# Attention and two MLP layers on one core: the order of the MLP part handed to the framework's scheduler

## The chip, the cores and the metric

The kernel runs on one core of a Trainium2 chip. The metric is the device time of one execution in microseconds. A core has five engines that matter here: TensorE (PE, matmuls; PEld is its weight load), VectorE (DVE), ScalarE (ACT), GpSimd (POOL), and SyncE (SP), which here only issues DMA transfers. Each works through its own queue of instructions in order, and waits for the others through semaphores.

## What is computed

Sigmoid attention over 4 batches and 12 heads (S = 448, D = 64), then two MLP layers over 1792 tokens, all in fp32. The weights come as fp64 and are read as 64-bit integers.

```python
def _attn_ref(q, k, v):
    scores = q @ k.T / sqrt(64) - log(S)
    return sigmoid(scores) @ v
def _moe_ref(x, w_in, w_out):            # x: 1792 x 768, w_in: 768 x 2048, w_out: 2048 x 768
    h = x @ w_in
    r = np.maximum(h, 0.0)
    return (r * r) @ w_out
def _moe2_ref(x, w_in, w_out, alpha):
    h = x @ w_in
    g = np.maximum(h, 0.0) + alpha * np.minimum(h, 0.0)
    return g @ w_out
x = attention, transposed to 1792 x 768
out = _moe2_ref(_moe_ref(x, ...), ...)
```

## The kernel before

Attention takes the first 158.6 us; the MLP part is what the change touches. It runs in 32 units, n = 0 to 31: two layers, in each two halves of the tokens (p), in each 8 blocks of 256 columns of d_ff (fp). fp32 values are split into a high and a low word, and a product takes three matmuls (high by high, high by low, low by high).

A unit has two phases on TensorE. First come seven products of a Strassen-like scheme (`product(k)`, L396): 9 matmuls of 448 columns each, into three PSUM banks h0, h1, h2 in the order 0, 1, 2, 1, 2, 0, 1. ACT copies h0 to c21 (L588). The adds (L582, DVE) combine h1 and h2 with c21 into c12, c22 and c21, and a product may overwrite a bank only after its add has read it: product 3 needs the first add on h1, which needs c21. `hidden` then makes the activation g as two words: in layer 0 on ACT (relu L403, square L404, L405), in layer 1 on ACT (L411, L412), DVE (L415) and ACT (L416); the low word is DVE's L417. Then come the output products (`out_products`, L434), in pairs on two PSUM tiles o0 and o1: 72 matmuls of 448 columns in layer 0, 84 of 384 in layer 1. Each pair is collected by DVE into acc (L469; on ACT, L467, in the first block), and only then its tile can be written again.

Beside that each unit prepares later ones. The weights of the next unit: four sums (`weight_sum`, L123 to L129, DVE), then high words on ACT (L136) and low words on DVE (L137) of four pieces, called s12, a1, a2 and s34 (s12 and s34 are made of sums, a1 and a2 of words_i). The output weights: high word L495 (ACT), low word L499 (POOL, four pieces). Raw weights are loaded from DRAM (L86, L88, issued by SP) into two buffers called raw, scaled in two steps (L94, L96, ACT), joined into words_i or words_o (L103, DVE), and kept in DRAM (L105); later units recall them (L111). All raw weights, of both layers, are loaded and joined in attention and in units 0 to 14. The next half of the tokens is staged: ACT L158 and POOL L159 write a piece into the one `stage` tile, SP stores it (L505, kept_x), and units 7, 15 and 23 load it back as X. POOL also makes x sums (L151).

All code, attention and MLP, stands in one `with tc.manual_schedule():` block: the instructions of each engine run in the order in which the code issues them. The MLP code sets that order by hand: `at(step, ...)` puts a side job into one of 13 steps (i0 to i6 behind the seven products, o0 to o5 behind the output pairs), and `do(step)` issues it there.

Of the kernel before, what the change touches and what calls it, by code (L numbers as in the profile page):

```python
# [20 lines left out]
def fused_kernel(ctx: ExitStack, tc: tile.TileContext, q, k, v, w1i, w1o, w2i, w2o, alpha, out):  # L21
# [142 lines left out]
    with tc.manual_schedule():  # L164
# [206 lines left out]


        mpool = ctx.enter_context(tc.tile_pool(name="mpool", bufs=1, reuse_waits="tile"))
        psum = ctx.enter_context(tc.tile_pool(name="mpsum", bufs=1, space=bass.MemoryType.PSUM, reuse_waits="tile"))
        X.append(mpool.tile([P, 2, KH, S], F32R, name="x6"))
        e21, e22, e12, e11 = (mpool.tile([P, S], F32, name=f"c{s}") for s in ("21", "22", "12", "11"))
        pos = [mpool.tile([P, S], F32, name=f"pos{i}") for i in range(2)]
        WO = [mpool.tile([P, 2, DM], F32R, name=f"wo{j}") for j in range(2)]
        G = [mpool.tile([P, 2, PAIR], F32R, name=f"g{j}") for j in range(2)]
        acc.append(mpool.tile([P, NC * PAIR], F32, name="acc1"))  # L380
        stage = mpool.tile([P, 2, S], F32R, name="stage")
        two = [psum.tile([P, 2, 512], F32, name="o0")]
        hb = [psum.tile([P, 512], F32, name=f"h{i}") for i in range(3)]
        two.append(psum.tile([P, 2, 512], F32, name="o1"))
        BANK = (0, 1, 2, 1, 2, 0, 1)
        OPERAND = (0, 4, 3, 5, 6, 1, 2)
        HIGH, LOW = ((0, 0), (0, 1)), ((1, 0),)
        turns = {"pair": 0, "pos": 0, "x": 0}

        def product(k):  # L390

            ps = hb[BANK[k]][:, :S]
            for c in range(KH):
                at = OPERAND[k] * HALF + c * P
                for i, (wp, xp) in enumerate(((0, 0), (0, 1), (1, 0))):
                    nc.tensor.matmul(ps, W[:, wp, at:at + P], X[k][:, xp, c], start=(k < 3 and c == 0 and i == 0), stop=(c == KH - 1 and i == 2), skip_group_check=True)  # L396

        def hidden(n, src, e, j, t):

            layer, p, fp = UNITS[n]  # L400
            gh, gl = (G[j][:, i, t * S:(t + 1) * S] for i in range(2))
            if layer == 0:
                nc.scalar.activation(e, src, AF.Relu)  # L403
                nc.scalar.activation(gh, e, AF.Square)  # L404
                nc.scalar.activation(e, e, AF.Square)  # L405
                second = lambda: None
            else:
                f = 2 * fp + j
                up = pos[turns["pos"] % 2]
                turns["pos"] += 1  # L410
                nc.scalar.activation(up, src, AF.Relu)  # L411
                nc.scalar.activation(e, src, AF.Relu, scale=-1.0)  # L412

                def second():
                    nc.vector.scalar_tensor_tensor(out=e, in0=e, scalar=nal[:, f:f + 1], in1=up, op0=ALU.mult, op1=ALU.add)  # L415
                    nc.scalar.activation(gh, e, AF.Copy)  # L416
            return second, lambda: nc.vector.tensor_sub(gl, e, gh)  # L417

        def outputs(n):

            if UNITS[n][0] == 0:
                return [[(c, t), (c + 1, t)] for t in (1, 0) for c in range(0, NC, 2)]
            return [[(m, 0), (m, 1)] for m in reversed(range(NM))]

        def out_product(n, o, ps, j, ways, begin, end):

            for i, (gi, wi) in enumerate(ways):
                if UNITS[n][0] == 0:
                    c, t = o
                    ops = WO[j][:, wi, c * P:(c + 1) * P], G[j][:, gi, t * S:(t + 1) * S]  # L430
                else:
                    m, e = o
                    ops = G[j][:, gi, m * P:(m + 1) * P], WO[j][:, wi, e * HALF:(e + 1) * HALF]
                nc.tensor.matmul(ps, *ops, start=(begin and i == 0), stop=(end and i == len(ways) - 1), skip_group_check=True)  # L434

        def out_products(n):

            size = S if UNITS[n][0] == 0 else HALF
            pairs = []
            for os in outputs(n):  # L440
                both = two[turns["pair"] % 2][:, :, :size]
                turns["pair"] += 1
                pairs.append((os, both))
            for ways in (HIGH, LOW):
                for os, both in pairs[:2]:
                    for i in range(2):
                        out_product(n, os[i], both[:, i], 1, ways, ways is HIGH, False)
            for at, (os, both) in enumerate(pairs):
                for i in range(2):
                    if at < 2:  # L450
                        out_product(n, os[i], both[:, i], 0, HIGH + LOW, False, True)
                    else:
                        out_product(n, os[i], both[:, i], 0, HIGH + LOW, True, False)
                        out_product(n, os[i], both[:, i], 1, HIGH + LOW, False, True)
                collect(n, os, both)
                yield at

        def collect(n, os, both):
            layer, p, fp = UNITS[n]
            if layer == 0:  # L460
                c, t = os[0]
                part = values_of(p)[:, c:c + 2, t]
            else:
                m = os[0][0]
                part = acc[p][:, m * DM:(m + 1) * DM].rearrange("p (e c) -> p e c", e=2)
            if fp == 0:
                nc.scalar.activation(part, both, AF.Copy)  # L467
            else:
                nc.vector.tensor_add(part, both, part)  # L469
            if fp == NB - 1 and layer == 1:  # L470
                if n == NU - 1:
                    for e in range(2):
                        store(p * PAIR + m * P, acc[p][:, m * DM + e * HALF:m * DM + (e + 1) * HALF], slice(e * HALF, (e + 1) * HALF), (nc.sync, nc.scalar))
                else:
                    store(p * PAIR + m * P, acc[p][:, m * DM:(m + 1) * DM])

        def store(col, rows, channels=slice(0, DM), queues=(nc.sync,)):

            i = at_queue = 0
            while i < P:  # L480
                b, at = divmod(col + i, S)
                to = out[b * S:(b + 1) * S, channels]
                if at < MAIN:
                    r, p = divmod(at, P)
                    n = min(P - i, P - p)
                    to = to[:MAIN].rearrange("(p r) c -> p r c", r=R)[p:p + n, r, :]
                else:
                    n = min(P - i, S - at)
                    to = to[at:at + n, :]
# [17 lines left out]
        for n in range(NU):  # L507
# [8 lines left out]
            def do(step):  # L516
                for job in todo.get(step, ()):
                    job()
# [134 lines left out]
```

## Time and profile before

| | |
|---|---|
| median of 3 runs | 1223.83 us (1223.69 to 1228.6) |
| the profiled execution | 1226.25 us, span 1224.5 us, mean granted clock 0.968 |
| TensorE matmuls busy | 1105.6 us (90%) |
| DVE / ACT / POOL busy | 772.1 / 604.8 / 274.8 us |
| L396, product matmuls | 2016, busy 435.9 us |
| L434, output matmuls | 1344 of 384 columns, busy 271.5 us; 1152 of 448 columns, busy 252.5 us; 48 of the latter take 9.99 us in a row |
| L495 (ACT) and L499 (POOL), mean of one | 836 ns, 1226 ns |

The difference between the profiled execution's time and its span, 1.75 us, lies around the span. A wait of an engine is the idle time right before an instruction, with what ended it. Idle time of an engine that is not the bottleneck costs nothing by itself.

### The profile page before, as it was taken

Reading aid. Unit: us, or ns where it says so; the run is one execution under the profiler, and the core shown is the slowest. Engines: PE = TensorE matmul, PEld = TensorE weight load, DVE = VectorE, ACT = ScalarE, POOL = GpSimd, SP = SyncE. Lnnn points to the kernel's source line nnn. Section 1 sums busy time; section 2 is a strip of 40 time slices with the busy share of each in tenths; the row PEclk is TensorE's granted clock in tenths of the full one; section 3 lists DMA queues with packets and bytes.
Section 4 is the critical chain, followed back from the end, with each engine's and each line's share of the span. In section 5 each row is a group of like instructions: output and inputs, shape, how many; then the busy total and the mean of one; then the engine's idle time right before and its main releaser. Section 6 shows DMA issues by size and latency. Waiting matters only on the chain.

```text
span 1224.5 us, 14729 instructions
## 1 busy us (share of the span) xinstructions
PE 1105.6 (90%) x5607; PEld 932.5 (76%) x5607; DVE 772.1 (63%) x990; ACT 604.8 (49%) x933; POOL 274.8 (22%) x229
## 2 busy tenths in 40 slices
PE   9999999889898789888889899899899899999998
PEld 5555578778787678777678788788788888888888
DVE  5458866577677556657666646666665646656664
ACT  5577767555455576555454554333332352333332
POOL 0012212323423022323423212231322211101011
PEclk9999999899899989989899999999999999999999
DMA  7677455455656755656556412221226411111102
GB/s 155 152 199 198 148 196 167 165 173 166 199 164 220 282 208 196 220 193 225 199 199 217 172 52 97 67 82 63 73 69 247 142 52 40 41 50 52 52 26 90
DMA packets 126006, 174.77 MB, mean 143 GB/s; under 512 B 55536, under 2 KB 98800, under 8 KB 124272
## 3 DMA queue, kind: packets, MB, share of 16 engines
q1 hardware_dynamic: 123440, 172.59, 43.5%
q10 hardware_dynamic: 2496, 1.25, 0.4%
q8 instruction: 44, 0.72, 0.2%
q14 instruction: 26, 0.21, 0.1%
HBM read 123.87 MB, written 49.94 MB: 142 GB/s over the span
## 4 chain that ended last, share of the span: by engine, by line
PE 37%; DVE 25%; ACT 19%; DMA 12%; issue 5%; POOL 1%; SPq 1%; ACTq 0%; DVEq 0%
PE o L434 17%; PE h L396 11%; DMA kept_x<-stage 4%; ACT wi L136 4%; PE av L265 3%; DVE c L582 3%; DVE c L415 3%; PE sc L245 3%; DVE sums L125 3%; DVE acc L469 3%; DVE wi L137 2%; ACT g L416 2%; DVE g L417 2%; ACT g L404 2%; ACT c L412 2%
## 5 line engine op out<-in xcount | busy, mean ns | idle before, releaser
L396 PE MATMUL h<-x,wi 128*128 128x448 f32 x2016 | 435.9, 377 | 34.1 <-DVE c L582 34.1
L396 PEld LDWEIGHTS h<-x,wi 128*128 128x128 f32 x2016 | 390.5, 194 | 74.1 <-DVE c L582 37.5
L434 PE MATMUL o<-wo,g 128*128 128x384 f32 x1344 | 271.5, 355 | 45.6 <-DVE acc L469 27.6
L434 PEld LDWEIGHTS o<-wo,g 128*128 128x128 f32 x1344 | 245.5, 199 | 70.1 <-ACT wi L136 25.3
L434 PE MATMUL o<-g,wo 128*128 128x448 f32 x1152 | 252.5, 371 | 32.2 <-DVE acc L469 19.2
L434 PEld LDWEIGHTS o<-g,wo 128*128 128x128 f32 x1152 | 211.6, 188 | 70.4 <-DVE acc L469 20.1
L499 POOL TENSOR_TENSOR wo<-words_o,wo 128x384 fp32r<-128x384 f32 x128 | 152.7, 1226 | 354.9 <-ACT wo L495 354.7
L469 DVE TENSOR_TENSOR acc<-o,acc 128x768 f32<-128x768 f32 (+1 forms) x182 | 184.5, 1015 | 73.3 <-PE o L434 72.0
L582 DVE TENSOR_TENSOR c<-h,c 128x448 f32<-128x448 f32 x160 | 98.9, 618 | 144.4 <-PE h L396 83.2
L137 DVE TENSOR_TENSOR wi<-sums,wi 128x768 fp32r<-128x768 f32 x64 | 61.2, 957 | 109.5 <-ACT wi L136 109.5
L159 POOL TENSOR_TENSOR stage<-acc,stage 128x448 fp32r<-128x448 f32 x36 | 41.2, 1145 | 363.0 <-ACT stage L158 363.0
L417 DVE TENSOR_TENSOR g<-c,g 128x448 fp32r<-128x448 f32 x128 | 88.7, 693 | 3.6 <-ACT g L416 1.9
L588 ACT ACTIVATE c<-h 128x448 f32<-128x448 f32 x32 | 17.2, 538 | 148.5 <-PE h L396 137.8
L247 ACT ACTIVATE a<-sc,bias 128x896 f32<-128x896 f32 x72 | 69.1, 1005 | 35.6 <-PE av L265 22.6
L416 ACT ACTIVATE g<-c 128x448 fp32r<-128x448 f32 x64 | 37.0, 578 | 78.0 <-DVE c L415 77.9
L137 DVE TENSOR_TENSOR wi<-words_i,wi 128x768 fp32r<-128x768 f32 x64 | 48.4, 757 | 40.2 <-ACT wi L136 40.2
L403 ACT ACTIVATE c<-c 128x448 f32<-128x448 f32 x48 | 27.5, 573 | 73.8 <-DVE c L582 73.8
L411 ACT ACTIVATE pos<-c 128x448 f32<-128x448 f32 x48 | 27.2, 568 | 73.5 <-DVE c L582 73.5
L158 ACT ACTIVATE stage<-acc 128x448 fp32r<-128x448 f32 x36 | 20.5, 571 | 84.8 <-DMA kept_x<-stage 84.8
L265 PE MATMUL av<-a,v 128*64 128x448 f32 x288 | 59.4, 548 | 0.0
L151 POOL TENSOR_TENSOR acc<-acc 128x448 f32<-128x448 f32 x40 | 57.3, 1450 | 0.1
L136 ACT ACTIVATE wi<-sums 128x768 fp32r<-128x768 f32 x64 | 53.0, 829 | 0.0
(166 smaller groups left out, 989.5 us busy)
## 6 DMA issues: line engine op xcount, KB each, us to landing
kept_x<-stage SPq DMA_DIRECT2D x36, 448.0 KB, 2.9
x<-kept_x SPq DMA_DIRECT2D x12, 1344.0 KB, 8.4
v<-in_v_dram SPq DMA_DIRECT2D x24, 192.0 KB, 2.9
nat<-in_q_dram SPq DMA_DIRECT2D x22, 192.0 KB, 3.5
nat<-in_k_dram SPq DMA_DIRECT2D x20, 192.0 KB, 3.3
late<-held SPq DMA_DIRECT2D x12, 224.0 KB, 2.2
acc<-late SPq DMA_DIRECT2D x1, 2688.0 KB, 9.4
out_dram<-acc SPq DMA_DIRECT2D x14, 192.0 KB, 2.7
```

The costliest lines, as they stand in the source:

```text
L136: nc.scalar.activation(hi, w, AF.Copy)
L137: nc.vector.tensor_sub(lo, w, hi)
L151: eng.tensor_sub(to[c], x[c], y[c])
L247: nc.scalar.activation(sig[u, j], ps[:, :, :S], AF.Sigmoid, bias=bias[:, :1], scale=SCALE)
L265: nc.tensor.matmul(avs[u][h * D:(h + 1) * D, :S], vals[u][:, h, j, :], a[:, h, :], start=(u % 2 == 0 and j == 0), stop=(u % 2 == 1 and j = ...
L396: nc.tensor.matmul(ps, W[:, wp, at:at + P], X[k][:, xp, c], start=(k < 3 and c == 0 and i == 0), stop=(c == KH - 1 and i == 2), skip_group ...
L416: nc.scalar.activation(gh, e, AF.Copy)
L417: return second, lambda: nc.vector.tensor_sub(gl, e, gh)
L434: nc.tensor.matmul(ps, *ops, start=(begin and i == 0), stop=(end and i == len(ways) - 1), skip_group_check=True)
L469: nc.vector.tensor_add(part, both, part)
L499: nc.gpsimd.tensor_sub(WO[j][:, 1, at], words["o"][:, j, at], WO[j][:, 0, at])
L582: nc.vector.tensor_add(to, hb[bank][:, :S], other)
```

## The change

The `manual_schedule` block now ends with attention. The MLP code stands outside it, with one indentation less and otherwise unchanged, so the framework's scheduler sets the order of every engine's queue there. The instructions and their number stay the same; the line numbers behind line 371 go down by one (L396 becomes L395, L469 L468, and so on).

```diff
@@ -369,257 +369,256 @@
             values(2 * ND - 1)
             finish(2 * ND - 1)
 
-
-        mpool = ctx.enter_context(tc.tile_pool(name="mpool", bufs=1, reuse_waits="tile"))
-        psum = ctx.enter_context(tc.tile_pool(name="mpsum", bufs=1, space=bass.MemoryType.PSUM, reuse_waits="tile"))
...
+    mpool = ctx.enter_context(tc.tile_pool(name="mpool", bufs=1, reuse_waits="tile"))
+    psum = ctx.enter_context(tc.tile_pool(name="mpsum", bufs=1, space=bass.MemoryType.PSUM, reuse_waits="tile"))
...
```

DVE, a unit of layer 1 before, from the second add on h1 to the second accumulation (c_1787 is c22, c_1788 c12, c_1789 c11, c_1786 c21; the first L137 is s12, the second a1):

```order
L582 TENSOR_TENSOR c_1787<-h_1800,c_1787 128x448
L127 TENSOR_TENSOR sums<-words_i 128x384
L129 TENSOR_TENSOR sums<-words_i,sums 128x384
L582 TENSOR_TENSOR c_1788<-h_1801,c_1788 128x448
L415 SCALAR_TENSOR_TENSOR c_1787<-c_1787,nal,pos_1790 128x448
L137 TENSOR_TENSOR wi<-sums,wi 128x768
L417 TENSOR_TENSOR g_1795<-c_1787,g_1795 128x448
L415 SCALAR_TENSOR_TENSOR c_1788<-c_1788,nal,pos_1791 128x448
L582 TENSOR_TENSOR c_1786<-h_1800,c_1786 128x448
...
L469 TENSOR_TENSOR acc_76<-o_1802,acc_76 128x768
...
L137 TENSOR_TENSOR wi<-words_i,wi 128x768
L469 TENSOR_TENSOR acc_76<-o_1798,acc_76 128x768
```

The same place now (all numbers one higher: c_1788 is c22, c_1789 c12, c_1790 c11, c_1787 c21):

```order
L137 TENSOR_TENSOR wi<-sums,wi 128x768
L581 TENSOR_TENSOR c_1788<-h_1801,c_1788 128x448
L581 TENSOR_TENSOR c_1789<-h_1802,c_1789 128x448
L414 SCALAR_TENSOR_TENSOR c_1788<-c_1788,nal,pos_1791 128x448
L137 TENSOR_TENSOR wi<-sums,wi 128x768
...
L137 TENSOR_TENSOR wi<-words_i,wi 128x768
L414 SCALAR_TENSOR_TENSOR c_1787<-c_1787,nal,pos_1792 128x448
L468 TENSOR_TENSOR acc_76<-o_1803,acc_76 128x768
L468 TENSOR_TENSOR acc_76<-o_1799,acc_76 128x768
L416 TENSOR_TENSOR g_1796<-c_1787,g_1796 128x448
```

s12 and s34 have moved forward between the adds, a1 and c21's L414 stand ahead of the first accumulation, and the four sums have gone to later accumulations.

TensorE, the output phase of a unit of layer 1 now (o is one of the two output tiles, x_70 with h_1800 is product 0 of the next unit):

```order
L433 MATMUL o_1799<-wo_1793,g_1795 128x384 x6
L433 MATMUL o_1803<-wo_1793,g_1795 128x384 x6
L395 MATMUL h_1800<-x_70,wi 128x448 x2
L433 MATMUL o_1799<-wo_1793,g_1795 128x384 x3
```

Two matmuls of the next unit's product 0 stand behind the first two output pairs; before, all nine stood behind the last pair. In layer 0 it is one to five of them.

ACT, layer 0, from the end of unit 2 into unit 3, before (raw4i and raw4o are raw weights of unit 4, c_1786 is c21):

```order
L94 ACTIVATE raw4i_2383<-raw4i_2383 128x768
L158 ACTIVATE stage<-acc_1796 128x448
L96 ACTIVATE raw4i_2383<-raw4i_2383 128x768
L158 ACTIVATE stage<-acc_1796 128x448
L588 ACTIVATE c_1786<-h_1799 128x448
L495 ACTIVATE wo_1793<-words_o 128x768
L495 ACTIVATE wo_1792<-words_o 128x768
```

And now (c_1787 is c21):

```order
L96 ACTIVATE raw4i_2384<-raw4i_2384 128x768
L158 ACTIVATE stage<-acc_1797 128x448 x2
L94 ACTIVATE raw4o_2469<-raw4o_2469 128x768
L494 ACTIVATE wo_1793<-words_o 128x768
L494 ACTIVATE wo_1794<-words_o 128x768
L96 ACTIVATE raw4o_2469<-raw4o_2469 128x768
L587 ACTIVATE c_1787<-h_1800 128x448
```

The first scale of raw4o and both wo now stand ahead of c21. In the other units of layer 0 it reads alike, without the stage pieces. On SP the load that this scale needs stands behind two stores of the stage and the store of the joined raw4i:

```order
L504 DMA kept_x_2_1806<-stage 256x1x448
L504 DMA kept_x_1_1805<-stage 256x1x448
L105 DMA kept4i_2467<-words_i 128x768
L88 DMA raw4o_2469<-in_moe_w_out_dram 128x768
```

On DVE the two joins of raw i (L103) stood at the head of their unit, ahead of the two adds that read h1 and h2 first. They now stand between the accumulations of the unit before, and the two joins of raw o are what stands around the first add. DVE, around the start of unit 3, now:

```order
L103 SCALAR_TENSOR_TENSOR words_o<-raw4o_2469 128x768
L581 TENSOR_TENSOR c_1789<-h_1801,c_1787 128x448
L103 SCALAR_TENSOR_TENSOR words_o<-raw4o_2484 128x768
L581 TENSOR_TENSOR c_1788<-h_1802,c_1787 128x448
```

The sums of unit 1 and the scaling of its raw output weights moved forward into the last part of attention.

## Rows read from the trace of the kernel before

**Rows 1.** Waits of TensorE: engine, line, waited for: total us, times, longest.

```profile
PE o L434 <- DVE acc L469: 46.8, 46, 2.3
PE h L396 <- DVE c L582: 34.1, 9, 7.2
```

**Rows 2.** Busy time by stage: window, us, engines' busy us, clock, DMA share, GB/s.

```profile
188.66:420.31 231.65, 205.88 (x947) 178.90 (x945) 159.94 (x192) 131.69 (x205) 68.02 (x52) 0.97 0.57 190
420.31:458.33 38.02, 30.44 (x136) 27.20 (x135) 19.42 (x25) 25.51 (x38) 8.89 (x7) 0.87 0.61 207
458.33:665.54 207.21, 179.71 (x811) 156.92 (x810) 136.26 (x161) 111.94 (x173) 63.33 (x48) 0.95 0.61 207
665.54:796.02 130.48, 118.33 (x577) 106.41 (x576) 78.18 (x106) 56.81 (x97) 30.93 (x27) 0.97 0.29 105
796.02:928.17 132.15, 120.37 (x589) 109.30 (x589) 83.37 (x112) 47.81 (x83) 37.27 (x32) 0.96 0.22 76
928.17:997.40 69.23, 60.64 (x295) 55.32 (x295) 38.91 (x56) 30.94 (x53) 12.85 (x11) 0.95 0.48 165
997.40:1192.10 194.70, 178.33 (x883) 161.81 (x883) 119.44 (x167) 67.14 (x115) 25.68 (x24) 0.97 0.14 45
```

**Rows 3.** TensorE's timeline, last unit: start, us, instruction, count.

```profile
1205.12 15.05 PE L434 MATMUL o<-wo,g 128*128 128x384 f32 x84
```

**Rows 4.** TensorE's timeline, two units of layer 1, with waits in brackets.

```profile
1095.54 13.18 PE L396 MATMUL h<-x,wi 128*128 128x448 f32 x63
1108.56 1.56 PE L434 MATMUL o<-wo,g 128*128 128x384 f32 x8
...
1118.80 8.56 PE L434 MATMUL o<-wo,g 128*128 128x384 f32 x48 [2.24 <-DVE acc L469]
...
1150.45 10.15 PE L434 MATMUL o<-wo,g 128*128 128x384 f32 x48 [2.26 <-DVE acc L469]
```

**Rows 5.** All engines in the first of these units, DVE's rows.

```profile
1108.75 0.96 DVE L137 TENSOR_TENSOR wi<-sums,wi 128x768 fp32r<-128x768 f32 x1 [2.46 <-ACT wi L136]
...
1113.16 0.96 DVE L469 TENSOR_TENSOR acc<-o,acc 128x768 f32<-128x768 f32 x1
...
1114.76 0.69 DVE L415 SCALAR_TENSOR_TENSOR c<-c,nal,pos 128x448 f32<-128x448 f32 x1
...
1116.83 0.96 DVE L137 TENSOR_TENSOR wi<-words_i,wi 128x768 fp32r<-128x768 f32 x1 [1.38 <-ACT wi L136]
...
1117.70 0.95 DVE L469 TENSOR_TENSOR acc<-o,acc 128x768 f32<-128x768 f32 x1
```

**Rows 6.** Busy time by window, the two units apart.

```profile
1095.50:1127.20 31.70, 28.98 (x149) 26.23 (x148) 20.07 (x28) 11.05 (x19) 4.28 (x4) 1.00 0.16 51
1127.20:1160.40 33.20, 30.46 (x148) 27.71 (x148) 20.07 (x28) 11.06 (x19) 4.28 (x4) 0.95 0.15 48
```

**Rows 7.** TensorE's timeline, end of unit 16.

```profile
717.35 10.73 PE L434 MATMUL o<-wo,g 128*128 128x384 f32 x60 [1.30 <-ACT acc L467]
```

**Rows 8.** All engines in unit 2, layer 0.

```profile
221.53 0.90 ACT L94 ACTIVATE raw3i<-raw3i 128x768 f32<-128x768 f32 x1
...
225.87 0.58 ACT L158 ACTIVATE stage<-acc 128x448 fp32r<-128x448 f32 x1 [3.45 <-DMA kept_x<-stage]
...
227.14 0.52 ACT L588 ACTIVATE c<-h 128x448 f32<-128x448 f32 x1
...
228.37 9.94 PE L396 MATMUL h<-x,wi 128*128 128x448 f32 x36 [4.32 <-DVE c L582]
```

**Rows 9.** DMA issues: KB each, median us from issue to landing.

```profile
kept_x<-stage SPq DMA_DIRECT2D x36, 448.0 KB, 2.9
...
raw4i<-in_moe_w_in_dram SPq DMA_DIRECT2D x2, 768.0 KB, 5.3
...
raw7o<-in_moe_w_out_dram SPq DMA_DIRECT2D x2, 768.0 KB, 7.1
```

**Rows 10.** Waits of ACT: total us, times, longest.

```profile
ACT stage L158 <- DMA kept_x<-stage: 84.8, 18, 7.6
```

More of the change, by code (lines that the diff above doesn't have):

```diff
@@ L379, in fused_kernel @@
[L379 to L387, printed above, removed]
@@ L419, in outputs @@
[L419 to L434, printed above, removed]
@@ L436, in out_products @@
[L436 to L489, printed above, removed]
-                queues[at_queue % len(queues)].dma_start(out=to, in_=rows[i:i + n])
-                at_queue += 1
-                i += n
@@ new lines, in fused_kernel @@
+    G = [mpool.tile([P, 2, PAIR], F32R, name=f"g{j}") for j in range(2)]
+    acc.append(mpool.tile([P, NC * PAIR], F32, name="acc1"))
+    stage = mpool.tile([P, 2, S], F32R, name="stage")
+    two = [psum.tile([P, 2, 512], F32, name="o0")]
+    hb = [psum.tile([P, 512], F32, name=f"h{i}") for i in range(3)]
+    two.append(psum.tile([P, 2, 512], F32, name="o1"))
+    BANK = (0, 1, 2, 1, 2, 0, 1)
+    OPERAND = (0, 4, 3, 5, 6, 1, 2)
+    HIGH, LOW = ((0, 0), (0, 1)), ((1, 0),)
+    turns = {"pair": 0, "pos": 0, "x": 0}
@@ new lines, in out_products @@
+    def out_products(n):
+        size = S if UNITS[n][0] == 0 else HALF
+        pairs = []
+        for os in outputs(n):
+            both = two[turns["pair"] % 2][:, :, :size]
+            turns["pair"] += 1
+            pairs.append((os, both))
+        for ways in (HIGH, LOW):
+            for os, both in pairs[:2]:
+                for i in range(2):
+                    out_product(n, os[i], both[:, i], 1, ways, ways is HIGH, False)
+        for at, (os, both) in enumerate(pairs):
+            for i in range(2):
+                if at < 2:
+                    out_product(n, os[i], both[:, i], 0, HIGH + LOW, False, True)
+                else:
+                    out_product(n, os[i], both[:, i], 0, HIGH + LOW, True, False)
+                    out_product(n, os[i], both[:, i], 1, HIGH + LOW, False, True)
+            collect(n, os, both)
+            yield at
@@ new lines, in collect @@
+    def collect(n, os, both):
+        layer, p, fp = UNITS[n]
+        if layer == 0:
+            c, t = os[0]
+            part = values_of(p)[:, c:c + 2, t]
+        else:
+            m = os[0][0]
+            part = acc[p][:, m * DM:(m + 1) * DM].rearrange("p (e c) -> p e c", e=2)
+        if fp == 0:
+            nc.scalar.activation(part, both, AF.Copy)
+        else:
+            nc.vector.tensor_add(part, both, part)
+        if fp == NB - 1 and layer == 1:
+            if n == NU - 1:
+                for e in range(2):
+                    store(p * PAIR + m * P, acc[p][:, m * DM + e * HALF:m * DM + (e + 1) * HALF], slice(e * HALF, (e + 1) * HALF), (nc.sync, nc.scalar))
+            else:
+                store(p * PAIR + m * P, acc[p][:, m * DM:(m + 1) * DM])
```

309 lines of the change are left out of this document (168 added, 141 removed).

## The prediction

> **What bounds the kernel now.** I read the total waits of TensorE first, then the span cut into stages, then its timeline inside one unit of each kind, and last the other engines at the places where it waits. I number the 32 units of the MLP part n = 0 to 31; 0 to 15 are layer 0, 16 to 31 layer 1. TensorE is the bound everywhere: in the waits of the whole run two rows stand out, 46.8 us at L434 for the accumulation (L469) that has to empty a PSUM pair, and 34.1 us at L396 for the DVE adds (L582) that have to empty h1 and h2 [rows 1]. By stage [rows 2], units 1 to 7 take 231.65 us (33.1 each), unit 8 alone 38.02, units 9 to 14 207.21 (34.5), units 15 to 18 130.48, units 19 to 22 132.15 (33.0), units 23 and 24 69.23, units 25 to 30 194.70 (32.45). The last unit shows what TensorE needs when nobody makes it wait: its 84 output matmuls take 15.05 us [rows 3]; 63 product matmuls take about 13.0 (the step from 1095.54 to the outputs, [rows 4]). That is 28.1 us in layer 1. Layer 0 has 72 wider output matmuls, near 15.0 to 15.4 us (48 take 9.99 in the table), so about 28.9 with small gaps. Everything between 28 to 29 and 32 to 35 us is waiting, so an order that has TensorE wait less can gain up to some 4 us in a unit, and nothing else is there to gain: the instructions are the same.
>
> **Layer 1, the ten units (19 to 22 and 25 to 30) in which the new order has neither raw loads nor stage pieces nor X reloads.** In the unit that starts at 1095.54 TensorE waits 2.24 us at 1118.80 [rows 4] for the second accumulation. DVE's rows say why [rows 5]: the first accumulation runs at 1113.16, then an L415 at 1114.76, then L137 of a1 stands at the head of the queue and waits 1.38 us for ACT's high word, and the accumulation behind it starts only at 1117.70, about 4 us after its pair of products was done. Before that, L137 of s12 had waited 2.46 us at 1108.75, because ACT makes s12's high word behind the activations of c12. In every second unit or so the clock then falls: the 48 matmuls after the wait take 8.56 us in one unit and 10.15 in the next [rows 4], and the window of the second has a mean clock of 0.95 against 1.00 [rows 6].
>
> In the new order s12 is made on ACT ahead of the activations; s12's and s34's L137 stand between adds, a1's and c21's operations ahead of the first accumulation, and the two first accumulations follow each other directly. I walked the unit by hand, each instruction starting when its engine and its inputs are free, with 0.6 to 0.69 us for a DVE operation of 448 columns, 0.96 for L137 and L469 [rows 5] and 0.5 to 0.6 for ACT's of 448 columns (0.52 in [rows 8]). From the end of the two product matmuls pulled ahead, the other 61 end at 12.7, the first 24 output matmuls at 17.05, two matmuls of the next unit at 17.45. DVE ends c21's L414 at 17.4 and the first accumulation at 18.4, so TensorE waits 1.05 us here and no longer 2.24 later. The second accumulation ends at 19.3 and nobody waits for it, since its pair is wanted at 20.7. The four weight sums, which stood among the adds, now come between later accumulations; they need the recalled weights (about 24) and push the fifth accumulation to 27.3, which costs 0.35 us. Period: 13.0 + 15.05 + 1.05 + 0.35 + 0.15 of refill = 29.6. The bounds are 28.1 (no wait) and 31.7 (the 2.24 us stay). Whether the clock falls: after a wait of 1.30 us in unit 16, 60 matmuls of this size take 10.73 us [rows 7], the 0.179 each of the last unit, so I take no fall. **Term: 132.15 - 4 x 29.6 = -13.8, and 194.70 - 6 x 29.6 = -17.1.**
>
> The Trainium skill ("TensorE: Matmul & The Clock Gate", "A second HAM failure mode: psum-queue depth-cycling") says that a kernel which goes round its PSUM banks idles TensorE briefly between groups of matmuls, and that the clock then goes up and down. By that page the wait of 1.05 us, which stays in each unit, would keep the fall: 1.6 us in half of ten units, 8 us less gain. The row of unit 16 speaks against it.
>
> **Layer 0 with raw loads, units 1 to 7.** Today TensorE waits once a unit in front of product 3, e.g. 4.32 us at 228.37 [rows 8]: product 3 overwrites h1, whose add needs c21, and ACT had c21 (227.14) behind two stage pieces, of which the second waited 3.45 us for the transfer of the first. In units without stage pieces the joins of raw i, which stand ahead of the adds on DVE, do the same more cheaply. The change puts both joins of raw i between the accumulations of the unit before, so the adds lose that obstacle. But it also puts the scale (L94) of raw o0 ahead of both wo and c21 on ACT; raw o0's load goes out when the join of raw i0 has freed its buffer, behind its store on SP, and lands some 6 us later (between the 5.3 and 7.1 of [rows 9]). Then L94 (0.90 [rows 8]), two wo at 0.8 (the mean of L495 is 836 ns in the table), L96 and c21 follow, so c21 is done 5 to 6 us into the unit and the add after 6.5, where product 3 wants it at 5.6; a join of raw o1 delays the second add as well. I take 2 us of waiting: 31 us a unit, between 29 (loads land early) and 37. At the ends of units 1, 2 and 3 two stage pieces stand ahead of that L94 on ACT and both kept_x ahead of that load on SP. Each costs a round of ACT, POOL and a transfer of 2.9 us [rows 9], about 5.5 us in all: 36.5. **Term: 4 x 31 + 3 x 36.5 - 231.65 = +2, between -25 and +28.**
>
> **Unit 8.** The 38.02 us hold the longest product wait of all, 7.2 us [rows 1]: ACT first waits for the raw loads of the next unit, then makes c21. With these loads out earlier and behind less, 33: **-5**, between -9 and 0.
>
> **Units 9 to 14** load raw weights of the second layer through two buffers, twice a unit; load, scale, join and store go round twice in about 24.5 us plus queueing. My walks give 33.1 with a 3 us wait for a join between two accumulations, and 31.7 to 32.5 without. I take 33.0: 198 - 207.2 = **-9**, between -25 (30.4 each) and +12 (36.5 each).
>
> **Units 15 to 18, 23, 24.** In 16 and 17 the remaining stage pieces stand on ACT before c21: +2.5 and -0.5; 15 and 18 -1 and -4 with the layer 1 pattern, together **-3**. Unit 23 (X reloads) loses most of its product wait, **-5.5** with 24. Bounds -10 and +8.
>
> **Attention and the ends.** Four scales of raw (0.90 each) and four sums of unit 1 move into attention's tail; most of it stands beside TensorE's work: **+1.5**, between 0 and 6. Unit 0 and unit 31: 0.
>
> The Trainium skill ("SBUF — State Buffer", "Summary: rules for kernel authors") says that a DVE operation with two SBUF inputs and a GpSimd operation that reads SBUF shut each other out, so that the second waits for the whole first. L137 of s12 now falls beside POOL's L499, and by that page it could wait 1.2 us (the mean of L499 on the page of the profile is 1.226). The add behind it frees h1 for product 6, some 3.7 us later in the walk, so the sum would stay; it makes the slower rival a little likelier in layer 0, where that slack is already spent.
>
> **Sum.** -13.8 - 17.1 + 2 - 5 - 9 - 3 - 5.5 + 1.5 = -49.9. The profiled execution took 1226.25 us, so 1176.4 in its terms; the median of the runs is 2.4 below the profiled one: **1174**.
>
> **Rivals.**
> (a) *ACT and SP queue behind loads, slower.* If L94 of raw o0 waits for its load throughout, c21 comes after some 10 us into each unit instead of 5 to 6. For it: ACT already waits 84.8 us in all for kept_x at L158 [rows 10], and the new order puts more behind such waits. It decides where the load lands later than about 4 us into the unit. Then units 1 to 7 take 37.5 (+31), 9 to 14 37.5 (+18), 8 stays, 15 to 18 and 23 gain nothing, attention +3; layer 1 still gives its 31: 1223.8 + 31 + 18 + 3 - 31 = about 1245 if all go; slower than before from 31 of these 52 us on.
> (b) *Loads are never last.* Units 1 to 14 near 30, layer 1 at 29: -22, -8, -27, -37 and -8.5 for the others: about 1125 to 1140.
> (c) *The wait only moves.* DVE's first accumulations are released by the same activations as before, so TensorE waits 2.2 us at the earlier place and the clock falls as before: layer 1 gains nothing, layer 0 the 10 or so of the sum: 1215 to 1224. Against it: the 1.38 us for a1 have gone from between the accumulations. That the scheduler keeps the old order is excluded by the rows of the change.
>
> **How the numbers follow.** The forecast (1150 to 1205 on its own) 0.59, (a) 0.17, (b) 0.12, (c) 0.12. Eight in ten: leave out the larger part of (a) at the top and the lower half of (b) at the bottom, 1138 to 1224. A change of 0.5% (6 us) is about what a measurement of this kernel tells from none. Faster by more: forecast, (b) and about half of (c), 0.77; within: the other half of (c) and a little of (a), 0.09; slower, the rest of (a), 0.14.
>
> **What would show it.** In the changed trace: units 25 to 30 at 29 to 30 us, one wait of about 1 us before the third pair, none over 2 us, clock 1.00 there (right for layer 1; 31 or more is wrong). In units 2 to 4, product waits of 5 us or more behind L158 and L94 on ACT; in 5 to 7 about 2. If units 5 to 7 and 9 to 14 also wait 5 us or more with ACT at an L94, (a) holds.

## The result and the profile after

The changed kernel takes 1111.86 us (median of 4 runs, 1106.94 to 1112.72), 0.907 of the time before (95% interval 0.903 to 0.910). The profiled execution took 1106.94 us, with a span of 1105.2 us and a clock of 0.993. The forecast of 1174 us had the sign right and held 50 of the 112 us of the gain; the time lies below the range. By stage, in us, from the profiled executions (1226.25 and 1106.94 us, so the stages together give 119 us and not the 112 of the medians):

| stage | before | forecast | after |
|---|---|---|---|
| attention, unit 0 | 188.7 | 190.2 | 194.8 |
| units 1 to 7 | 231.7 | 233.5 | 212.7 |
| unit 8 | 38.0 | 33.0 | 33.2 |
| units 9 to 14 | 207.2 | 198.0 | 178.6 |
| units 15 to 18 | 130.5 | 127.5 | 122.0 |
| units 19 to 22 | 132.2 | 118.4 | 110.3 |
| units 23 and 24 | 69.2 | 63.7 | 56.4 |
| units 25 to 30 | 194.7 | 177.6 | 165.2 |

The same view as [rows 2], of the changed kernel (window, us, busy us of PE, PEld, DVE, ACT, POOL, then clock, DMA share, GB/s):

```profile
194.84:407.50 212.66, 197.56 (x946) 175.41 (x945) 159.74 (x189) 125.21 (x208) 69.60 (x54) 1.00 0.60 207
...
440.72:619.27 178.55, 169.88 (x810) 149.88 (x808) 133.03 (x161) 105.73 (x171) 54.80 (x43) 1.00 0.69 228
...
741.25:851.55 110.30, 110.30 (x590) 105.57 (x589) 76.78 (x112) 43.53 (x77) 15.72 (x16) 1.00 0.19 58
...
907.98:1073.21 165.23, 165.23 (x882) 158.14 (x882) 112.47 (x163) 65.87 (x116) 23.58 (x24) 1.00 0.18 53
```

In units 19 to 22 and 25 to 30 TensorE's busy time is the whole window: it never waits there, and the clock is 1.00 where it was 0.96 and 0.97. In layer 0 TensorE is still idle for 2.2 us a unit (units 1 to 7) and 1.4 us (units 9 to 14). The waits of TensorE, as [rows 1]:

```profile
PE h L395 <- DVE c L581: 12.5, 14, 2.1
PE o L433 <- DVE acc L468: 12.3, 14, 2.1
PE o L433 <- ACT g L415: 5.8, 2, 4.3
```

The 46.8 us for the accumulations are 12.3, the 34.1 us for the product adds 12.5. One unit of layer 1 on TensorE, as [rows 4]: the two pulled matmuls stand between the first 24 output matmuls and the other 60, and there is no wait in brackets anywhere.

```profile
990.49 12.76 PE L395 MATMUL h<-x,wi 128*128 128x448 f32 x61
1003.09 4.33 PE L433 MATMUL o<-wo,g 128*128 128x384 f32 x24
1007.25 0.57 PE L395 MATMUL h<-x,wi 128*128 128x448 f32 x2
1007.66 10.56 PE L433 MATMUL o<-wo,g 128*128 128x384 f32 x60
```

### The profile page after: what moved, and what is told of

It reads as the page before. It is cut to its first block, busy times and chain, and to the rows that moved or that the text cites. A ratio compares the mean times of both kernels' runs of the same rounds, so it can differ in the third digit from the quotient of the medians.

```text
span 1105.2 us, 14871 instructions
## 1 busy us (share of the span) xinstructions
PE 1057.4 (96%) x5607; PEld 911.7 (82%) x5607; DVE 764.2 (69%) x990; ACT 587.4 (53%) x933; POOL 271.6 (25%) x229
## 3 DMA queue, kind: packets, MB, share of 16 engines
q10 hardware_dynamic: 2496, 1.25, 0.4%
## 4 chain that ended last, share of the span: by engine, by line
PE 52%; issue 13%; DMA 11%; ACT 10%; POOL 8%; DVE 5%; SPq 0%; ACTq 0%; POOLq 0%; DVEq 0%
PE o L433 24%; PE h L395 18%; PE av L265 4%; POOL wo L498 4%; PE sc L245 3%; DMA kept_x<-stage 3%; POOL stage L159 2%; ACT wi L136 1%; POOL acc L151 1%; POOL x L159 1%; ACT c L404 1%; ACT c L402 1%; DVE acc L468 1%; ACT g L403 1%; PE scr L255 1%
## 5 line engine op out<-in xcount | busy, mean ns | idle before, releaser
L395 PE MATMUL h<-x,wi 128*128 128x448 f32 x2016 | 429.4, 368 | 16.8 <-DVE c L581 12.5
L395 PEld LDWEIGHTS h<-x,wi 128*128 128x128 f32 x2016 | 376.3, 188 | 59.3 <-DVE c L581 19.0
L433 PE MATMUL o<-g,wo 128*128 128x448 f32 x1152 | 245.0, 369 | 14.4 <-DVE acc L468 11.8
L498 POOL TENSOR_TENSOR wo<-words_o,wo 128x384 fp32r<-128x384 f32 x128 | 138.7, 1115 | 461.9 <-ACT wo L494 461.9
L433 PE MATMUL o<-wo,g 128*128 128x384 f32 x1344 | 241.6, 337 | 7.1 <-ACT g L415 5.8
L433 PEld LDWEIGHTS o<-wo,g 128*128 128x128 f32 x1344 | 235.1, 189 | 10.9 <-ACT g L415 6.6
L468 DVE TENSOR_TENSOR acc<-o,acc 128x768 f32<-128x768 f32 (+1 forms) x182 | 184.2, 1015 | 58.0 <-PE o L433 57.2
L494 ACT ACTIVATE wo<-words_o 128x768 fp32r<-128x768 f32 x64 | 51.0, 838 | 168.7 <-PE o L433 132.5
L416 DVE TENSOR_TENSOR g<-c,g 128x448 fp32r<-128x448 f32 x128 | 80.5, 644 | 30.6 <-ACT c L404 29.4
L136 ACT ACTIVATE wi<-sums 128x768 fp32r<-128x768 f32 x64 | 53.6, 839 | 44.9 <-PE h L395 44.7
L137 DVE TENSOR_TENSOR wi<-sums,wi 128x768 fp32r<-128x768 f32 x64 | 69.0, 1081 | 7.4 <-ACT wi L136 6.5
L137 DVE TENSOR_TENSOR wi<-words_i,wi 128x768 fp32r<-128x768 f32 x64 | 52.5, 830 | 14.5 <-ACT wi L136 14.5
L414 DVE SCALAR_TENSOR_TENSOR c<-c,nal,pos 128x448 f32<-128x448 f32 x64 | 43.5, 680 | 8.8 <-ACT c L411 8.6
L159 POOL TENSOR_TENSOR x<-acc,x 128x448 fp32r<-128x448 f32 x15 | 21.9, 1478 | 102.4 <-ACT x L158 102.4
```

Source lines behind the costliest of these rows:

```text
L136: nc.scalar.activation(hi, w, AF.Copy)
L137: nc.vector.tensor_sub(lo, w, hi)
L159: eng.tensor_sub(lo, x, hi)
L498: nc.gpsimd.tensor_sub(WO[j][:, 1, at], words["o"][:, j, at], WO[j][:, 0, at])
```

## The experiments

Times of units are read from each run's profiled execution; where a run was timed more than once, its median and its ratio to the kernel before stand with it.

**Which layer.** The end of the manual block was put at unit 16, or its start.

```diff
     for n in range(NU):
+        if n == NU // 2:
+            manual.close()              # l1_sched; l0_sched opens the block here instead
```

> The order by hand is kept through unit 15 and only units 16 to 31 are left to the scheduler. From the two traces units 16 to 31 went from 527.0 to 456.1 us. Theory A (the gains of the two layers are independent): 1226 - 71 = about 1155 us, units 25 to 30 at 27.6 us each. Rival B (what layer 1 gains rests on what layer 0 left done, the stored pieces and recalled weights): 1165 to 1185, units 16 to 18 near their old 33 us.

> The converse: scheduler through unit 15, the order by hand from unit 16 on. From the two traces attention with unit 0 lost 6.2 us and units 1 to 15 went from 508.8 to 454.3. Theory A: 1226 - 48 = about 1178 us, units 25 to 30 at 32.4 us with the fallen clock in every second one. Rival B: 1190 or more, or units 25 to 30 different from 32.4.

Measured: l1_sched 1155.1 us (ratio 0.942, 0.940 to 0.944), units 25 to 30 at 27.54; l0_sched 1182.0 us (0.963, 0.961 to 0.965), units 25 to 30 at 32.45, as before. The ratios' gains add up to 0.095, the changed kernel's is 0.093: the layers are independent, theory A holds, and each can be studied alone.

**Layer 1: which part of the order.** First the edits that the prediction's working named, by hand in the kernel before.

```diff
-                at("i4", lambda: weight_parts("s12"))
+                at("i2" if layer else "i4", lambda: weight_parts("s12"))      # h_s12
-                at("o0", lambda: weight_parts("a1"))
+                at("i5" if layer else "o0", lambda: weight_parts("a1"))       # and this: h_s12_a1
...
+                if layer and M < NU:                                          # h_sums, its i2 and i3 left out
+                    for s in range(4):
+                        at("o5", lambda s=s: weight_sum(s))
```

> The order by hand, one edit in layer 1: s12 (ACT's high word, DVE's low word) is issued at step i2, right behind its sums and ahead of the activations of c22 and c12, and no longer at i4. Read in units 25 to 30. Theory D (the queues of ACT and DVE stand behind s12: DVE's 2.46 us wait for it delays all that the first accumulations need): the 2.24 us wait of TensorE falls below 1 us, no fall of the clock, units near 29.5 us. Theory E (the wait is a1's alone, its L137 waits for ACT between the two accumulations): units stay at 32.45 on average. Theory P (what ends the wait are the matmuls that TensorE pulls from the next unit): no change here.

> As h_s12, and a1 at step i5, ahead of c21's activations and of both accumulations, as the scheduler has it. Theory D: little more than h_s12, under 0.5 us a unit. Theory E: only here do units fall, to 30 us or less. Theory P: a wait of about 1 us stays in front of the third pair, units at 29 to 30.

> The order by hand, another single edit in layer 1: the four sums stand at the end of the unit before, behind its accumulations, and no longer between the adds. They take 2.9 us of DVE, of which 0.7 because of POOL's L499 beside them. Theory D: little, units at 31.5 to 32.5, since s12's place sets the delay. A rival (DVE is simply full in front of the first accumulation): 30 us or less.

> The three edits together, TensorE's order as before. Theory P: a wait stays in front of the third pair, about 1 us by the walk of the prediction, units at 29 or more. Theories D and E: no wait left, units at 27.6 to 28.0 as in the changed kernel, without pulling a matmul ahead.

Measured, units 25 to 30: h_s12 31.4 or 33.0, wait 2.26 us; h_s12_a1 32.0 to 34.2; h_sums 31.6 or 33.2, wait 2.23; all three together 30.0 and 31.25, that is 1.8 less than before, with a wait of 1.83 us for a low word (L417) inside the first two pairs. Theories D and E fall: an edit alone moves the wait or leaves it. Theory P can't be judged here: no wait stands in front of the third pair, but a longer one stands ahead of it; h_rest below comes back to it. With a1 ahead, TensorE waits 3.04 us for a low word (L417) that now stands behind a1's L137:

```profile
1052.04 0.58 ACT L416 ACTIVATE g<-c 128x448 fp32r<-128x448 f32 x1 [0.76 <-DVE c L415]
...
1054.24 0.96 DVE L137 TENSOR_TENSOR wi<-words_i,wi 128x768 fp32r<-128x768 f32 x1 [2.24 <-ACT wi L136]
...
1055.65 0.62 DVE L417 TENSOR_TENSOR g<-c,g 128x448 fp32r<-128x448 f32 x1
...
1056.33 1.10 PE L434 MATMUL o<-wo,g 128*128 128x384 f32 x4 [3.04 <-DVE g L417]
```

The first of these rows is the hint. ACT's L416 waits 0.76 us for DVE, and so it does for 62 of the 64 activations of layer 1 in the run of before, 77.9 us in all. In the hand order ACT makes relu and negative part of one tensor, waits while DVE combines them (L415), copies the result (L416), and only then takes the next tensor, while DVE waits for ACT. In the scheduler's order the copy stands behind the first two operations of the next tensor. That edit (what is cut below also takes c11's low word and c21's L415 from behind the first accumulation to ahead of it, as the scheduler has them):

```diff
             add(e12, 2, e12)
-            second22()                       # DVE's L415, then ACT's copy
+            mid22()                          # DVE's L415 alone
             second12, low12 = hidden(n, e12, e12, 0, 1)
+            copy22()                         # ACT's copy, behind the next tensor's two
...
```

> The order by hand, one edit in layer 1: ACT's last copy of each activation (L416) stands behind the first two operations of the next one, and L415 stands ahead of the previous low word on DVE, as the scheduler has them; s12, a1, the sums and TensorE as before. Theory I (ACT and DVE wait for each other in turn, 77.9 us at ACT's L416 in the run of before, and the wait of TensorE is the end of that chain): units 25 to 30 at 28 to 29.5 us, no wait over 1 us. Rival M (the wait is made in several places, each of which alone holds the accumulations back): 31 us or more, with a wait of about 2 us that has another releaser.

Measured: units 25 to 30 at 29.55 us, clock 1.00, no wait over 0.35 us; the whole kernel 1184.8 us beside 1225.8. That is theory I, at the upper end of what it expected. Of the 32.45 us a unit the edit takes 2.9, and the fall of the clock goes with the 2.2 us wait. ACT's waits for L415 (L414 in the lower two rows), in the kernel before, in h_inter and in the changed kernel:

```profile
ACT g L416 <- DVE c L415: 77.9, 62, 2.8
ACT g L415 <- DVE c L414: 33.3, 47, 1.4
ACT g L415 <- DVE c L414: 9.8, 13, 0.8
```

What it shortens in the unit is the stretch between the first two accumulations. In the kernel before [rows 5] the first starts 17.6 us into the unit, in h_inter (unit from 1002.96) 17.7; a1's high word (ACT, L136), for which the second has to wait behind a1's L137, starts at 20.4 and 18.3 us, and the second accumulation at 22.2 and 20.0. The first row is the kernel before, the others are h_inter:

```profile
1115.97 1.24 ACT L136 ACTIVATE wi<-words_i 128x768 fp32r<-128x768 f32 x2
...
1020.05 0.68 DVE L414 SCALAR_TENSOR_TENSOR c<-c,nal,pos 128x448 f32<-128x448 f32 x1 [0.19 <-ACT c L412]
1020.65 0.95 DVE L468 TENSOR_TENSOR acc<-o,acc 128x768 f32<-128x768 f32 x1
...
1021.25 1.24 ACT L136 ACTIVATE wi<-words_i 128x768 fp32r<-128x768 f32 x2
```

No run has the interleaving without the two moved instructions. With c21's L414 behind the first accumulation (0.95 us), it and a1 would come about 1 us later by these rows (an estimate), so a part of the 2.9 us may be theirs. One unit's output phase on TensorE in that run (behind the edit the lines are one lower):

```profile
1015.97 1.56 PE L433 MATMUL o<-wo,g 128*128 128x384 f32 x8
1017.72 1.32 PE L433 MATMUL o<-wo,g 128*128 128x384 f32 x6 [0.19 <-DVE g L416]
1019.38 2.03 PE L433 MATMUL o<-wo,g 128*128 128x384 f32 x10 [0.34 <-DVE g L416]
1021.66 11.01 PE L433 MATMUL o<-wo,g 128*128 128x384 f32 x60 [0.25 <-DVE acc L468]
```

Then the rest: s12, s34, a1, a2 and the sums where the scheduler has them, on top of the interleaving. A first version (h_full) wrote s34 before product 4 had read it, so that product 4 used the next unit's piece and TensorE waited 3.10 us for it in each unit; its 33.5 us a unit say nothing on the question, and h_rest is the mended one.

```diff
             step(4)
+            do("s34hi")                      # h_full had it ahead of step(4)
             add(e12, 2, e12)
             mid22()
+            do("s34lo")
...
+                    product(0, 0, 2)         # h_rest_pull: behind the second output pair
```

> The interleaving of h_inter together with s12, s34, a1, a2 and the sums where the scheduler has them, by hand; TensorE's order is that of before, nothing pulled ahead. If the order on ACT and DVE is the whole cause: units 25 to 30 at 27.6 to 28.0 us, clock 1.00. Theory P (the two pulled matmuls cover a wait that is left): a wait of 0.4 us or more in front of the third pair, units at 28.2 or more.

> The order by hand, layer 1: h_inter together with s12, s34, a1, a2 and the sums where the scheduler has them (in h_full s34 was written before product 4 had read it, here behind). TensorE's order is that of before. If ACT's and DVE's order is the whole cause: units 25 to 30 at 27.6 to 28.0 us, against 29.55 with the interleaving alone. If the two pulled matmuls cover a wait (theory P): a wait of 0.4 us or more in front of the third pair, units at 28.2 or more.

> h_rest (units 25 to 30 at 28.3 us, a wait of 0.43 us in front of the third pair) with one more edit: in layer 1 the first two matmuls of the next unit's product 0 are issued behind the first two output pairs, as the scheduler has them. If they are what is left: 27.6 us and no wait, that is 0.7 us a unit, more than the two matmuls' 0.41 us since the matmuls start again without a gap. If something else is left (the order of POOL's or ACT's wo): 28.3 again, with the wait at another place.

Measured: h_rest 28.3 us with a wait of 0.43 us in front of the third pair, h_rest_pull 27.88 without it, the scheduler 27.54. So layer 1's gain of 4.9 us a unit is 2.9 (interleaving), 1.25 (the weights' pieces and sums), 0.4 (the pulled matmuls, which is what theory P is right about), and 0.3 that stay open. The shares hold for this order of the edits: h_s12_a1_sums, pieces and sums without the interleaving, gave 1.8. The waits in front of the third pair:

```profile
1010.77 10.67 PE L435 MATMUL o<-wo,g 128*128 128x384 f32 x60 [0.43 <-DVE acc L470]
```

```profile
1003.46 0.57 PE L400 MATMUL h<-x,wi 128*128 128x448 f32 x2
1004.04 10.69 PE L437 MATMUL o<-wo,g 128*128 128x384 f32 x60
```

**Layer 0: what the raw weights cost.** `load`, `scale` and `join` return at once for n above 1.

> The kernel before without the raw weights from unit 2 on: their loads, scales, joins and stores are left out, and the weights of unit 0 and 1 are used throughout. Theory A (layer 0 lost its time to the ring of raw weights, whose loads end late in the hand order): units 2 to 7 fall from 33.6 us to 30 or below, units 9 to 14 from 34.5 to 30 or below. Rival C (layer 0 lost its time to the same DVE order as layer 1, ring or not): units 2 to 7 at 32 or more.

> The changed kernel without the raw weights from unit 2 on, as in nl_before. Theory A: units 2 to 7 fall from 30.4 us to 28.9 or less, within 1.5 us of nl_before, so that the orders differ little once the ring is gone. Rival C: nl_before stays 2 us a unit above this one.

Measured: without them the kernel before takes 27.8 to 28.0 us in units without stage pieces next to c21, and 28.8 to 31.0 in units 2, 5, 10 and 13 with them; the changed kernel 27.1 to 27.7 in units 2 to 6 and 10 to 14. So theory A holds in the main: with the raw weights gone the orders differ by some 0.3 us a unit, except where stage pieces stand. In units 1, 8 and 9 the scheduler's order is then the slower one (29.5, 29.75 and 31.5 us against 27.9 to 28.0). With the raw weights, the kernel before pays some 5 us a unit in units 1 to 7 and 9 to 14, and the changed one about 2. Units 2 and 3 of nl_before, then unit 3 of nl_after:

```profile
218.03:249.01 30.98, 29.18 (x137) 26.58 (x136) 19.39 (x23) 12.95 (x22) 12.71 (x10) 0.94 0.13 51
249.01:276.79 27.78, 27.78 (x136) 25.12 (x135) 17.30 (x23) 11.81 (x20) 10.20 (x8) 1.00 0.07 27
```

```profile
255.42:283.09 27.67, 27.67 (x138) 25.47 (x136) 16.85 (x23) 10.71 (x20) 3.94 (x4) 1.00 0.00 1
```

**Layer 0: joins, ring or stage pieces.** By hand in the kernel before: the joins of raw i moved to the end of the unit before (g_join); all loads, scales and joins half a unit earlier, with the output weights' words and a2 earlier too (g_ring); the stage pieces, and POOL's x sums that are issued with them, spread over the unit (g_stage); the last two together.

```diff
+                    at("o4", lambda: join(U, "i", 0))                          # g_join
+                    at("o5", lambda: join(U, "i", 1))
...
+                at("o2", lambda: join(U, "i", 0), lambda: load(U, "o", 0))     # g_ring, with its scales
+                at("o3", lambda: join(U, "i", 1), lambda: load(U, "o", 1))     # and joins of raw o at i0 to i2
...
-                    for step in ("o2", "o3", "o4", "o5"):                      # g_stage, layer 0
+                    for step in ("i2", "i6", "o2", "o4"):
                         at(step, waiting.pop(0))
```

> The order by hand, one edit in layer 0: the joins of raw i stand at the end of the unit before (o4, o5) and no longer ahead of the adds; loads and scales stay. Theory J (the joins ahead of the adds are the product waits): units 3 to 7 fall from 33.3 to 31 us or less. Theory R (the whole ring of raw weights is late: scaled at the end of a unit, joined at once): the wait only moves, 33 us or more, since the accumulations or the next adds now wait for the scales.

> The order by hand, layer 0: the whole ring half a unit earlier, as the scheduler has it: raw i joined between the accumulations, raw o loaded right behind each join, scaled at the head of the next unit and joined there, and raw i of the next loaded behind that. Stage pieces, sums and TensorE as before. Theory R: units 4 to 7 at 30 to 31 us and units 9 to 14 at 31 or less. If the rest of the scheduler's order makes the gain (sums behind the accumulations, matmuls pulled ahead): 32.5 or more. Unit 2 is a transition and slower.

> The order by hand, one edit in layer 0: the stage pieces stand at steps i2, i6, o2 and o4, no two behind each other, and no longer at o2 to o5 ahead of the next unit's c21. Theory T (c21 waits on ACT for the pieces, of which the second waits for the transfer of the first): units 2, 3, 5, 6 and 7, 33.4 to 35.4 us, fall to the 30.4 of unit 4. Theory R (the ring): they stay at 33 or more, now held by the joins of raw i.

> g_ring and g_stage together. In g_ring the raw loads landed early, but c21 stood on ACT behind two stage pieces, which waited 8.9 and 4.2 us for transfers. If ring and pieces hold each other: units 4 to 7 at 30.5 us or less and units 9 to 14 at 31 or less, as in the changed kernel. If the hand-made ring has another fault: 33 or more, with a wait whose releaser names it.

Measured, units 3 to 7 on average (before 33.3): g_join 33.1, g_ring 36.4, g_stage 31.2, g_ring_stage 35.3. Moving the joins changes nothing (theory J falls). Spreading the stage pieces is what counts: units 1 to 7 go from 231.65 to 217.5 us, and TensorE's waits for the product adds from 34.1 to 9.0 us, of which 7.0 are unit 8's:

```profile
PE o L434 <- DVE acc L469: 41.2, 37, 2.7
PE o L434 <- DVE g L417: 32.9, 34, 3.1
PE h L396 <- DVE c L582: 9.0, 4, 7.0
```

Theory T holds there, but for unit 7 (33.9 us). Units 9 to 14 go to 196.4 only; units 11 and 14 stay at 35 to 36. In both ACT waits at an L94 for a load: 2.81 us in unit 11, ahead of a1's high word, and TensorE then waits 2.68 us for an accumulation that stands on DVE behind a1's low word; 4.38 us in unit 14, ahead of c21. The ring made by hand is worse than the old place, for reasons of its own, as a stretch of g_ring_stage shows: the store of a stage piece stands on SP behind the joins' stores, so that ACT waits 11.0 us for it ahead of c21, and then a join and two sums stand between two adds (L603) on DVE, 5.6 us apart:

```profile
359.36 0.58 ACT L158 ACTIVATE stage<-acc 128x448 fp32r<-128x448 f32 x1 [11.00 <-DMA kept_x<-stage]
...
364.89 0.61 DVE L603 TENSOR_TENSOR c<-h,c 128x448 f32<-128x448 f32 x1
...
365.86 1.89 DVE L103 SCALAR_TENSOR_TENSOR words_o<-raw7o 128x768 int32<-128x768 int32 x1 [0.36 <-POOL wo L499]
...
367.68 1.51 DVE L123 TENSOR_TENSOR sums<-words_i 128x384 f32<-128x384 f32 x1
...
370.52 0.61 DVE L603 TENSOR_TENSOR c<-h,c 128x448 f32<-128x448 f32 x1
...
371.19 2.09 PE L396 MATMUL h<-x,wi 128*128 128x448 f32 x9 [1.65 <-DVE c L603]
```

The sum L123, 0.55 us by itself, takes 1.51 here beside POOL's x sums. So g_ring and g_ring_stage don't tell what the scheduler's ring is worth; units 9 to 14, 178.6 us by the scheduler against 196.4 with the pieces spread, suggest that it is worth something; but the rest of the scheduler's order in layer 0 (sums, pulled matmuls) was not tried alone either, so that stays open.

**The two chains together, and attention.**

> The whole kernel in the order by hand, with the edits of h_rest (layer 1) and g_stage (layer 0) together, TensorE's order and the ring of raw weights as before. If the two are independent: 1226 - 58 - 26 = about 1142 us, 0.931 of the kernel before; that is some 84 of the 115 us that the scheduler gains, and what is left would be units 9 to 14 (ring), 23 and 24, and 0.7 us a unit in layer 1. If the stage pieces of layer 0 hold something in layer 1 as well: another sum.

> The changed kernel with unit 0 still in the order by hand, so that nothing of the MLP part moves into attention before it. Attention and unit 0 took 194.8 us in the changed kernel and 188.7 before, with a wait of 2.8 us at 132 and a fall of the clock behind it. If the moved scales and sums cause that: 188.7 again, and the whole 5 to 6 us shorter than the changed kernel, about 1101 to 1106. If unit 1 then waits for what unit 0 does late: no gain in the whole.

hand_two took 1140.7 us (0.929, 0.926 to 0.933), as the sum says: two orderings made by hand give 0.071 of the 0.093. In n0_hand attention ends at 158.8 us again, not 164.3, but unit 0 takes 33.6 instead of 30.5, with a 2.19 us wait of TensorE for a low word, so the expected 188.7 became 192.4. The whole took 1103.25 us (1101.62 to 1105.86), 0.899 (0.898 to 0.901). Its interval and that of the changed kernel do not overlap, though they were not timed side by side; it is the fastest version here. What attention lost in the changed kernel: ACT's L94 of unit 1's raw output weights waits 5.1 us for its load at the head of ACT's queue, the sigmoid behind it comes late, TensorE waits 2.8 us, and the clock falls after it: 0.61 from 132 to 140 us, where the kernel before has 1.00.

```profile
129.36 0.88 ACT L94 ACTIVATE raw1o<-raw1o 128x768 f32<-128x768 f32 x1 [5.06 <-DMA raw1o<-in_moe_w_out_dram]
...
130.94 0.98 ACT L247 ACTIVATE a<-sc,bias 128x896 f32<-128x896 f32 x1
...
131.98 0.74 PE L245 MATMUL sc<-qkh 64*128 64x448 f32 x2 [2.81 <-ACT a L247]
```

## Why the prediction was wrong

*What bounds the kernel* held: TensorE's waits are the whole matter, and the instructions cost the same. The estimate of 28.1 us for layer 1 and 28.9 for layer 0 without waits was a little high (27.54, and 27.5 to 27.7 in nl_after): the last unit's 84 output matmuls take 15.04 us in the changed kernel too, those of the other units about 14.6. So even the lower bounds of the terms, 28.1 us a unit in layer 1 and 30.4 in units 9 to 14, were passed (27.54 and 29.8).

Between the profiled executions the sum says -49.9 us and the runs -119.3. Three terms make 61 of the 69 us between them: units 1 to 7 (21.0), layer 1 (20.4) and units 9 to 14 (19.7).

*Layer 1, term -30.9, measured -51.3.* The sign, the vanished fall of the clock (clock 1.00, as the row of unit 16 had said), and the early accumulations held. The rule of the Trainium skill ("TensorE: Matmul & The Clock Gate", "A second HAM failure mode: psum-queue depth-cycling") would have kept the fall; here the waits that bring it are gone. Where waits are left the trace agrees with it in part: of units 25 to 30 every second one has a clock of 0.95 with 2.2 us in the kernel before and with 1.83 us in h_s12_a1_sums, and all six have 1.00 with 0.43 us in h_rest. The step that failed is the walk, in size. Of the 2.06 us by which its 29.6 lie above 27.54, 1.05 and 0.35 are waits that did not come, 0.15 is the refill, and 0.5 the time without waits. (The 1.05 us are 0.95 by the walk's own 18.4 and 17.45.) It set every instruction behind the full duration of the one before, and so had the first accumulation start 17.4 us into the unit; the trace has 15.97. On one engine instructions start before the row of the one before has ended:

```profile
1001.79 0.53 ACT L410 ACTIVATE pos<-h 128x448 f32<-128x448 f32 x1
...
1002.22 0.53 ACT L411 ACTIVATE c<-h 128x448 f32<-128x448 f32 x1
1002.64 0.58 ACT L415 ACTIVATE g<-c 128x448 fp32r<-128x448 f32 x1
...
1004.99 0.95 DVE L137 TENSOR_TENSOR wi<-words_i,wi 128x768 fp32r<-128x768 f32 x1
...
1005.86 0.68 DVE L414 SCALAR_TENSOR_TENSOR c<-c,nal,pos 128x448 f32<-128x448 f32 x1
...
1006.46 1.96 DVE L468 TENSOR_TENSOR acc<-o,acc 128x768 f32<-128x768 f32 x2
```

ACT's 0.53 us operations are 0.43 apart and DVE's 0.95 and 0.68 us ones 0.87 and 0.60. Over a dozen instructions at about 0.1 us each this makes some 1.2 us, the size of the 1.05 us wait that was forecast; it is worked out so, no run isolates it. The cause that the walk began from was wrong too: it named L137 of a1 and s12, whose moves give nothing to speak of alone (32.2 us a unit with s12, 33.1 with both, 32.45 before); what had to come earlier was ACT's high word for a1, and the rows that mattered were those of L415 and ACT's waits around them.

*Layer 0, units 1 to 7, term +2, measured -19.0; units 9 to 14, -9 and -28.7.* The step that failed is the load of raw o0: units 2 to 4, put at 36.5 us for it, took 30.9, which makes 17 of the 21 us. I had it wait on SP behind both transfers of the two stage pieces at the end of the unit. Of the two kept_x rows ahead of it, the first belongs to an earlier piece. The trace of unit 2 into 3 (from 255.82):

```profile
246.69 0.56 ACT L158 ACTIVATE stage<-acc 128x448 fp32r<-128x448 f32 x1
...
249.01 0.52 SPq L504 DMA_DIRECT2D kept_x<-stage  x1
...
250.27 0.64 SPq L88 DMA_DIRECT2D raw4o<-in_moe_w_out_dram  x1
...
251.98 0.58 ACT L158 ACTIVATE stage<-acc 128x448 fp32r<-128x448 f32 x1 [4.73 <-DMA kept_x<-stage]
...
254.17 0.52 SPq L504 DMA_DIRECT2D kept_x<-stage  x1
...
256.26 0.91 ACT L94 ACTIVATE raw4o<-raw4o 128x768 f32<-128x768 f32 x1 [3.70 <-DMA raw4o<-in_moe_w_out_dram]
...
259.32 0.53 ACT L587 ACTIVATE c<-h 128x448 f32<-128x448 f32 x1
```

The load goes out at 250.27, between the two stores, and the L94 that needs it runs 0.44 us into the unit; c21 is done at 4.0 us instead of the 5 to 6 of the plain units, or over 10 with pieces. ACT's wait of 4.73 us for the first piece's transfer falls into the output phase, where TensorE does not wait for ACT. The mechanism of the stall before, c21 behind the pieces [rows 8], had been read rightly for unit 2; I then charged the other units' waits to the joins, which g_join refutes and g_stage corrects; and the wait is not there once a unit, but nine times in all [rows 1]. The 2 us of product waits that were forecast for a plain unit are 1.8 to 2.1 in units 2 to 4 and none in 5 to 7. (The lower bound of 29 us a unit gives -29, not -25.) In units 9 to 14 the 3 us wait for a join between two accumulations did not come: TensorE's longest wait there is 1.21 us. Rival (b), loads never last, came nearest; its terms add up to 1121, below the 1125 that it names, and that was still too high. The price of (a) never arose.

*Units 15 to 18, -3 and measured -8.5; 23 and 24, -5.5 and -12.8:* these units too have layer 1's order, and I had given them only part of its gain (unit 18 alone went from 34.85 to 27.58). Unit 17, not 16, is late: a stage piece on ACT waits 7.04 us for its transfer ahead of the activations, and TensorE then 4.25 us for L415, the third of its waits above. *Unit 8* met its term. *Attention, +1.5, measured +5.7:* the four scales were priced, the wait for their load at the head of ACT's queue was not; the bound of 6 held. The Trainium skill's rule on DVE and GpSimd shutting each other out ("SBUF — State Buffer", "Summary: rules for kernel authors") shows in the trace: L137 of the sums takes 1081 ns on average where it took 957, and single ones in layer 0 up to 1.91 us. In units 25 to 30, where the prediction looked for it, they take 0.94 to 0.96 us, as before, since POOL's L498 has ended by then (995.07 against 996.52 in the unit from 990.49); the sum did not hang on it.

## What to carry to other kernels

When two engines hand tensors to each other and both wait a little each time, look at the order in which they take turns before moving anything else: issuing the next tensor's first operations ahead of this one's last (with two instructions moved ahead of an accumulation) was worth 2.9 us of 32.45 here, and moving single waiting instructions was worth next to nothing. An instruction whose input comes from a transfer belongs where the engine has slack, not ahead of what frees the bottleneck's buffers; four pieces of staging moved within a unit gave 26 us. And a walk by hand should use the distance between starts, not durations, and should say for each store and load in a queue which piece it belongs to.

## What was not expected of the hardware

The same wait does not always cost the clock. In layer 1 of the kernel before, the 2.2 us wait was followed by the lower clock level in about every second unit (10.15 us instead of 8.56 for 48 matmuls), and so it was with 1.83 us in h_s12_a1_sums (0.95 and 31.25 us beside 1.00 and 30.0); in units 25 to 30 of h_inter, h_rest and the changed kernel, with waits of 0.43 us or none, the clock is 1.00. And on ACT and DVE an instruction starts up to 0.1 us before the row of the one before has ended, which a list of durations does not show.
